# K and Q stored as three rows per dimension, head packs loaded by one transfer, and the reciprocal broadcast cut in four, with another order table

## The chip, the cores and the metric

The kernel runs on one core of a Trainium2 chip. The metric is the time of one execution on the device in microseconds (us). The version before takes 1923.54 us, the median of three runs (1922.4 to 1924.5). Beside the runs stands one execution that was recorded with the hardware profiler; all durations of single instructions come from it. Engines are named as the profile names them: PE multiplies matrices (PEld is its loading of weights), DVE is the vector engine, ACT the scalar engine, POOL the third elementwise engine, and SP only issues transfers (DMAs). All DMAs of this kernel are issued by SP, one after the other; SP also does the waiting for them.

## The reference

The input x has 2048 rows (positions) of 640 numbers. The result is the sum of x, an attention block and a mixer block, both on the row-normalized x. Cut to what matters:

```python
xn = layernorm(x)
# attention, 32 heads of 20 dimensions
q, k, v = split(xn @ wqkv)
p = softmax(q @ k.T * 20 ** -0.5)
a = concat_heads(p @ v) @ wo
# mixer
h  = gelu(layernorm(xn) @ w1)            # four groups of columns shifted by +1, -1, +2, -2 positions
x1 = xn + shifted(h) @ w2
b  = x1 + gelu(layernorm(x1) @ w3) @ w4  # w3: 640 x 1536
return x + a + b
```

Everything is float32. The kernel multiplies with a shortened float32 type and so writes each operand as a high part plus a low part; a product is high*high + high*low + low*high.

## The kernel before

**Work.** Heads go in 16 pairs, and each pair in two blocks of 1024 queries, which makes 32 blocks. For a block, PE forms the scores twice: `pm` with queries on the partitions, over whose rows DVE takes maxima (`mx`), and, once the maximum is known, `s` with keys on the partitions, which ACT turns into `p` by the exponential. PE multiplies `p` with V (`pv`), whose output also holds the sums of `p`. All else (projections to K, Q and V, the mixer's four matrices, preparing weights, the final product with wo) is laid between the blocks' steps, so that PE has work when ACT or DVE lag.

**K and Q on their way.** A projection of 128 columns comes out of PE as `ps_k` or `ps_q`, is split into `hl` = (high, low), a tile of 128 x 2 x 512 with two buffers, and is stored to DRAM (`kd`, `qd`). A pack is what PE reads for a pair: `kpack` (two buffers, 2048 keys) and `zq` (three buffers, 1024 queries). Head e of the pair has partitions 64e to 64e+59: 20 dimensions, each three times. `SLOT_K` = (0, 0, 1) and `SLOT_Q` = (0, 1, 0) say which part stands in which of the three places: high, high, low for K, and high, low, high for Q, so that one product over 60 partitions makes the three terms at once. Two more partitions take the maxima (`zq<-md`). In the version before the three places are three blocks of 20 partitions, and `load_k` issues a DMA for each of them; `load_q` issues one for the first two and one for the third. A head that lies across two groups of 128 columns is loaded in two pieces, each by three DMAs.

**The sums.** At a block's end (`block_end`) the sums of `p` go to DRAM (`od<-ob`), come back spread over 128 partitions (`sm<-od`), DVE takes reciprocals (`rc`), which go to DRAM (`rcd<-rc`) and come back to every partition that needs them (`rb<-rcd`); POOL multiplies, and four DMAs store the result (`onm<-rb`).

**What sets the order.** A planner (`Plan.schedule`) runs over all operations with assumed costs and writes out a fixed order for each engine. The table `ORDER` decides what PE takes next: s (a score product), p (a product with V), m (a maximum product, counted apart only at places), d (anything that is due). A DMA has in the plan an issue cost on SP, a time `xfer` on one shared path, 1600 ns until it has landed, and an allowance `late` (3000 ns for prepared weights, `PREP`, and for the sums' chain, `LATE`; 1500 ns for packs). Eight DMAs may be under way; the ninth waits for the first. Engines take their instructions strictly in the planned order.

**Preparing weights.** `prep` loads a piece of a weight matrix (`ph_w<-in`), rounds it on ACT or DVE (`ph_w<-ph_w`), subtracts on POOL, and stores both parts (`wd_w<-ph_w`); later a DMA brings them to where PE reads them (`w_w<-wd_w`, `xT<-wd_w`). These casts stand in ACT's row between the exponentials.

Of the kernel before, what the change touches and what calls it, by code (L numbers as in the profile page):

```python
# [88 lines left out]
LATE = 3000.0  # L89
KB = 1  # L90
# [21 lines left out]
    "dsdsdddssppppssdsdddssdddssdddssddsddddsdsdddsddsdsddsdsdppppsddssddsdssddsdddsdsdsdddddsdsdsdppsssppdsddsdddd"
    "ddddsddsdddsssddddsddssddsddsdsdsddsdsppppssddsdsddsdsddsdddsdsdsddssddsdsddsdddssppppssdddssddsdsddddsdsddsdd"
    "ssdddsdsdsdsddpppssddddsddsdsddsdsddsdsdddddsspssdsdsdsdsddppppsddsddssddssdssdddddssddsdsdspssdppsspdssddsdsd"
    "psdddddsdsddddsddsdddssdddsddsddsdddsdsdddsdspppssddsddsddsddssddsdsdddsdsdppppsdsddsddsdsdsdddssdsdddddsddsds"
    "dsddsdsppppsdsddssdddsdssddddssddsdddssdsddsdsddspssspssddddsddsdddsdppdsdddssdsdsdsdsdsdsdddssppppssddsdsdsdd"
    "dsspdpssddddsdspdsdsdddsdpsddssdddssdsddsdsddsdddssddsdsdddssppppssdddssddsddsddsdsdsddddsssddddddsdssdddsdsdd"
    "sdsdppppssddsddsddsddsdssddsdddsdssddsppppsdsdsddsdsddsdsdddsddsdsdssdsdsdsddsdddssdpdpppsddssddssddsdsddsdsdd"
    "spssddpsdsppsdsdsddsdddsddddsdddddsdddsssdddddsdsddssdddssddsdsdppsssppsdsdsdsdddsdsddsdsdsdsddsdsppppsdsddsds"
    "dsdddsdsddsddsdsdddsdddsdsdsddsdspdpppssddddsdssddsdsddsdsddsdsdddsdsdsdsppppdsdssdddsdsddsdsdsdddddsssdddddsd"  # L120
    "ssdddsddsddsdsdpssspppddsdsddddddssddsdsdddssdddsdssddsddssppssdddsdsdddsspsspssspssspssspssspdssspssspssspsss"
    "pssddddsddsddddsdddddsssddddsdddddddsddsddddsddddsdddddsddsddppppsdsdddssdddsddsddddddddsddsddddsdddddddssdddd"
    "dsddddddddddsdsdddddsppppsdddsddddddsssdddddddsdsdddddddsddddddddsddppdddsddddsddddsddddsddsdddsdsdddsddddddds"
    "ppsddsdddddsddsddddsddssdddsdsdddsdsdddsddddddddddssddddpppsspssdddsdddsddsddddsdddssdddddsdddsdddsddddppsssps"
    "sspsddddsddsdddsddddsddssdddsdddsdddsdddsddddsdddddsddsppsssddppssdsdddddddsspddspssssspdpsdsdsddsdsdddddsddsd"
    "ddsssddddsdddddsdsdsddddddddsdsddsdddsdssddddpppppsdddsdsddddsdddddddsdddddsdsdddsddsddddssdddsddddsdsdddsddsd"
    "dspppsddddddsdsddddsddddssdddsdsddssdddsdsddsddssdppppssddsddsddssdddsdsdsdsdddssppppdsddsdssdddsdddssddsdddsd"
    "ddsdsddsddsdsdsddsdsdddsspppssdddsddsddsddsddsddsddsppppsddddsddddsdddsdsdddspsdsddssddsddsddssddsdsddsdsppsss"
    "ppdsdsddssdddssdddssdddsddssdsddsddsdsppppdsdsdsdsddsdsdddsdddsdsddsdsdsddsdsdsddsdsppppdssddsddsdsddsdsdsddds"
    "ddsddsddsddsdsdsdddsdddssdppppdsdddsddsdsdsdddsdsddddsdsdsddsdsddsdsppppsdsddssdddssdsddsddsddsddssdddsddssddp"  # L130
    "pppddsssddddsdsdsddsdddddsssddddsddssdddsdsdsddddssssppssppsssspssspssspssspsddsdsdddddsdsdddsdddssddsdddddsdd"
    "ssddddddssppppsdsddsdsdddddsddsddddssdsddddsddsddddsdddsdsppdsddddsddsdddsdddsdddsppsddsddsdsddddssddddddsddds"
    "ddddddsddddddssdddddddsdsdddddddddddddddsddppppdsdsddsdddddsdsdddddssddddsddsddsdddsddddssppppsdsdsdsdddsddddd"
    "sdsdddssddsddsdddddsdddsdddddddddssddpppddsdddddddsddsdddddsdpsdsdsdddsdddsdddsddsddsdddsddsddddsddddsdspssddp"
    "sddsdsddsdddsddsdddddsdddddddsdsppspssspssddpssspdsdddsddddsspsspddsssssspssspssddddsdsddssdddsdsdsddsdsppsdsd"
# [476 lines left out]
def tile_kernel(tc, x, wqkv, wo, w1, w2, w3, w4, out):  # L612
# [1002 lines left out]
```

## Time and profile before

| | |
|---|---|
| median of three runs | 1923.54 us |
| the profiled execution | 1928.14 us |
| its span, first to last instruction | 1926.4 us |
| PE busy | 97% of the span |
| DVE, ACT, POOL busy | 79%, 72%, 23% |
| mean granted clock of PE | 0.981 |
| DMA issues | 1355 |

PE's busy share is near the whole span, so what counts is where PE stands still and where its clock is lower than 1.00. A row of the view by stretches gives: the stretch (us from the span's start), its length, busy us of PE, PEld, DVE, ACT and POOL with their instructions, PE's granted clock, the DMA engines' mean busy share, and GB/s. A row of the chain of waits gives start, length and what the time went to; "DMA a<-b" there is the time from a DMA's issue to its landing as far as the next step waited for it. A row of the timeline gives start, length, engine, operation, tiles and count, and in brackets how long the engine stood idle before it and what ended that.

### The profile page before, as it was taken

The numbers are of one execution on the slowest core, as the hardware profiler recorded it, in microseconds if no ns is written. First come the engines' busy times: TensorE is split into PE (matmuls) and PEld (weight loads), VectorE is DVE, ScalarE is ACT, GpSimd is POOL, SyncE is SP. The second block draws the span as 40 slices with busy tenths as digits, with TensorE's granted clock in tenths as the row PEclk, the third lists the DMA queues.
The fourth block names the chain that finished last, engine by engine and source line by source line (L and its number), as shares of the span: only waits on it lengthen the run. The fifth ranks groups of instructions, "written<-read, shape, count | busy, mean of one in ns | idle before, by whom it ended". The sixth has DMA issues, their size and how long they took to land.

```text
span 1926.4 us, 44100 instructions
## 1 busy us (share of the span) xinstructions
PE 1861.3 (97%) x17153; PEld 1295.4 (67%) x17153; DVE 1512.6 (79%) x2691; ACT 1382.0 (72%) x2540; POOL 446.2 (23%) x663
## 2 busy tenths in 40 slices
PE   8999999998989999899999989999999999999998
PEld 7976676665665646566665757656677777776677
DVE  8998678886878888877778986768788877878734
ACT  5278667886877886668778666867777777777762
POOL 5012123423412333211111221101112222221211
PEclk9999999999999999999999999999999999999999
DMA  5664546536444586544424452233622323253502
GB/s 187 180 180 153 133 119 191 142 125 180 120 134 123 154 248 195 182 132 158 149 83 140 148 174 98 92 93 111 168 86 73 113 69 106 72 149 102 163 17 110
DMA packets 229425, 257.78 MB, mean 134 GB/s; under 512 B 57784, under 2 KB 172936, under 8 KB 229216
## 3 DMA queue, kind: packets, MB, share of 16 engines
q1 hardware_dynamic: 229216, 254.96, 44.3%
q8 instruction: 135, 2.21, 0.5%
q14 instruction: 74, 0.61, 0.1%
HBM read 151.64 MB, written 103.25 MB: 132 GB/s over the span
## 4 chain that ended last, share of the span: by engine, by line
PE 81%; DMA 10%; DVE 4%; ACT 2%; SPq 1%; issue 1%; POOL 1%; DVEq 0%; ACTq 0%; POOLq 0%
PE ps L356 23%; PE pv L356 20%; PE s L356 12%; PE pm L356 12%; PE psv L356 3%; PE pso L356 3%; DVE mx L324 3%; PE ps_q L356 3%; PE ps_k L356 3%; DMA kpack<-kd 2%; DMA ph_w<-in_B_w_dram 2%; SPq L324 1%; PE psl L356 1%; DMA zq<-qd 1%; DMA od<-ob 1%
## 5 line engine op out<-in xcount | busy, mean ns | idle before, releaser
L324 DVE TENSOR_REDUCE mx<-pm 128x1 f32<-128x512 f32 x2048 | 1271.3, 682 | 220.6 <-PE pm L356 127.2
L324 ACT ACTIVATE p<-s 128x512 f32<-128x512 f32 x2048 | 1109.1, 604 | 214.5 <-PE s L356 104.1
L356 PE MATMUL s<-zq,kpack 62*128 62x512 f32 x2048 | 759.0, 413 | 25.4 <-ACT p L324 10.9
L356 PE MATMUL pm<-kpack,zq 60*128 60x512 f32 x2048 | 761.8, 412 | 19.8 <-ACT p L324 13.4
L356 PE MATMUL pv<-p,v 128*32 128x512 f32 x4096 | 487.7, 601 | 2.8 <-ACT p L324 2.5
L356 PEld LDWEIGHTS s<-zq,kpack 62*128 62x128 f32 x2048 | 365.0, 188 | 131.8 <-DVE mx L324 33.1
L356 PEld LDWEIGHTS pm<-kpack,zq 60*128 60x128 f32 x2048 | 368.0, 188 | 117.5 <-ACT p L324 28.8
L356 PE MATMUL ps<-xT,w_w 64*128 64x512 f32 x2040 | 344.0, 401 | 5.4 <-DMA w_w<-wd_w 5.4
L356 PEld LDWEIGHTS pv<-p,v 128*32 128x32 f32 x4096 | 120.4, 109 | 237.2 <-issue 202.4
L356 PEld LDWEIGHTS ps<-xT,w_w 64*128 64x128 f32 x2040 | 222.8, 191 | 41.8 <-issue 10.4
L324 POOL TENSOR_TENSOR ob<-ob,obq 128x512 f32<-128x512 f32 x96 | 124.0, 1292 | 324.4 <-ACT obq L324 291.3
L356 PE MATMUL ps<-xT 64*128 64x320 f32 x1632 | 172.8, 308 | 0.0
L356 PEld LDWEIGHTS ps<-xT 64*128 64x128 f32 x1632 | 147.6, 186 | 12.1 <-issue 2.1
L324 ACT COPY obq<-pv 128x512 f32<-128x512 f32 x85 | 50.0, 588 | 129.4 <-PE pv L356 128.8
L356 PE MATMUL ps<-xT,gT 64*128 64x320 f32 x1152 | 123.1, 307 | 0.0
L344 POOL MEMSET scratch<- 1x1 f32 x134 | 12.3, 92 | 454.8 <-PE ps L356 273.7
L356 PEld LDWEIGHTS ps<-xT,gT 64*128 64x128 f32 x1152 | 104.8, 186 | 9.0 <-issue 3.4
L356 PE MATMUL psv<-wv,xT 64*128 64x320 f32 x960 | 93.9, 314 | 0.0
L356 PEld LDWEIGHTS psv<-wv,xT 64*128 64x128 f32 x960 | 83.3, 190 | 7.2 <-POOL scratch L344 1.4
L356 PE MATMUL ps_q<-xT,w_q 64*128 64x512 f32 x480 | 81.1, 398 | 0.0
L356 PE MATMUL ps_k<-xT,w_k 64*128 64x512 f32 x480 | 80.6, 399 | 0.0
L356 PE MATMUL pso<-wos,oT 64*128 64x320 f32 x768 | 67.0, 308 | 0.0
(180 smaller groups left out, 1382.4 us busy)
## 6 DMA issues: line engine op xcount, KB each, us to landing
kpack<-kd SPq DMA_DIRECT2D x78, 160.0 KB
w_w<-wd_w SPq DMA_DIRECT2D x48, 256.0 KB
gd<-pre SPq DMA_DIRECT2D x8, 1536.0 KB
g<-gd SPq DMA_DIRECT2D x64, 192.0 KB
wd_w<-ph_w SPq DMA_DIRECT2D x34, 320.0 KB
xT<-wd_w SPq DMA_DIRECT2D x34, 320.0 KB
zq<-qd SPq DMA_DIRECT2D x52, 160.0 KB
vd<-vst SPq DMA_DIRECT2D x32, 256.0 KB
```

Of the source, the lines that this page charges most:

```text
L324: o.insts = [getattr(e, m)(val(out), *[val(x) for x in ins], **{k: val(v) for k, v in kw.items()})]
L344: o.insts = [nc.gpsimd.memset(scratch.get(), 0.0)]
L356: o.insts = [nc.tensor.matmul(out.get(), lhsT.get(), rhs.get(), **kw) for out, lhsT, rhs, kw in products]
```

## The change

1. **Layout in DRAM.** `qd` and `kd` get the shape (128, 3, 2048): the three rows of a dimension stand next to each other in the order that the pack wants. `keep` stores a piece with two DMAs: one for both parts, and one that stores the high part a second time.
2. **Packs.** Partition 3*o + slot instead of 20*slot + o. A head is loaded by one DMA of 60 rows, a head across two groups by two. `place`, which builds the first pair's pack on the chip, is filled with step 3.
3. **Reciprocals.** `rb<-rcd` is four DMAs of 32 partitions each, every one from one row of 512.
4. **The planner's assumptions.** `dma` is told over how many DMA engines it spreads (`on`: for a pack the largest number up to 16 that divides its rows, 4 for `od`, 10 for `onm`); some issue costs and element sizes are other ones. The allowance for packs has a name and the same value.
5. **ORDER** is another table with the same counts of letters (4479 d, 2005 s, 512 p, 43 m). Of its rows two stand below.

```diff
+RLATE = 1500.0
 ORDER = (
...
-    "psddsddddddsssddddsddddddsddsdddddsddddsdddsdssdddddssdddddssddddsddddsdsdppppdsdsdsdddsddddsdddddsssdddddddsd"
+    "pdsddsdddddsssdddddddddssdddsdddddsdddsddddsddsdsdddssddddsddddsddsddsdsddppppsddsddddssddddsdddddsssddddsddds"
...
-    def dma(o, i, nbytes, es=2560, iss=None, **kw):
+    def dma(o, i, nbytes, es=2560, iss=None, on=16, **kw):
...
-                 xfer=1.1 * (8.0 + 0.0375 * es) * math.ceil(n / 16), **kw)
+                 xfer=1.1 * (8.0 + 0.0375 * es) * math.ceil(n / on), **kw)
...
-                b = 64 * h + slot * DH
-                pl("pool", 110.0, "tensor_copy", place[:, e, part, b:b + DH], ident[:, h * DH:(h + 1) * DH])
+                b = 64 * h + slot
+                pl("pool", 110.0, "tensor_copy", place[:, e, part, b:b + 3 * DH:3], ident[:, h * DH:(h + 1) * DH])
...
-    qd = [dt([P, 2, 2, HALF], F32R, f"qd{c}") for c in range(ND)]
-    kd = [dt([P, 2, 2, HALF], F32R, f"kd{c}") for c in range(ND)]
+    qd = [dt([P, 3, S], F32R, f"qd{c}") for c in range(ND)]
+    kd = [dt([P, 3, S], F32R, f"kd{c}") for c in range(ND)]
+    def keep(dst, k, tb, hl):
+        c = slice(tb * 512, (tb + 1) * 512)
+        dma(_f(dst[:, 1:3, c] if k else dst[:, 0:2, c]), _f(hl), 524288, 2048, 430.0)
+        return dma(_f(dst[:, 0 if k else 2, c]), _f(hl[:, 0, :]), 262144, 2048, 390.0)
...
-            dma(_f((qd, kd)[e][0][:, tb // 2, :, tb % 2 * 512:tb % 2 * 512 + 512]), _f(hl), 524288, 2048, 560.0)
+            keep((qd, kd)[e][0], e, tb, hl)
...
-                    for slot, part in enumerate(SLOT_K):
-                        b = 64 * e + slot * DH + o
-                        rdma(_f(t[b:b + n, s]).rearrange("p (c t) -> p c t", c=2), _f(src[r0:r0 + n, :, part, :]), n * S * 4, 4096)
+                    b = 64 * e + 3 * o
+                    rdma(_f(t[b:b + 3 * n, s]), _f(src[r0:r0 + n, :, s]).rearrange("p s t -> (p s) t"), n * S * 12, 8192, on=span(3 * n))
...
-                slots = list(enumerate(SLOT_Q))
-                if n == DH:
-                    b = 64 * e
-                    rdma(_f(t[b:b + 2 * DH, :]), _f(src[r0:r0 + n, qh]).rearrange("p q t -> q p t"), n * HALF * 8, 4096)
-                    slots = slots[2:]
-                for slot, part in slots:
-                    b = 64 * e + slot * DH + o
-                    rdma(_f(t[b:b + n, :]), _f(src[r0:r0 + n, qh, part, :]), n * HALF * 4, 4096)
+                b = 64 * e + 3 * o
+                rdma(_f(t[b:b + 3 * n, :]), _f(src[r0:r0 + n, :, qh * HALF:(qh + 1) * HALF]).rearrange("p s t -> (p s) t"),
+                     n * HALF * 12, 4096, on=span(3 * n))
...
-        adma(rb, rcd[blk].unsqueeze(1).to_broadcast([4, 32, 512]), 262144, LATE)
+        for r in range(4):
+            adma(rb[32 * r:32 * (r + 1), :], rcd[blk, r:r + 1].to_broadcast([32, 512]), 65536, LATE, iss=450.0)
```

What this does to the order of instructions shows best on SP. A row gives line, operation, the tile written and the tile read with their numbers, the shape written (partitions first), and xN for equal rows that follow each other.

SP before, where the packs of blocks 3 and of the second pair's K are loaded (`zq1`, `kpack0`), with the weight pieces `ph_q3` around them:

```order
L324 DMA ph_q3_0_3474<-in_A_wqkv_dram 128x2x128
L324 DMA zq1_79<-qd0_100 40x1x1024
L324 DMA zq1_79<-qd0_100 20x1024
L324 DMA zq1_79<-qd0_100 40x1x1024
L324 DMA zq1_79<-qd0_100 20x1024
L324 DMA ph_q3_1_3511<-in_A_wqkv_dram 128x2x128
L324 DMA kpack0_76<-kd0_105 20x2x1024 x6
L324 DMA vd1_111<-vst2_217 128x8x64
```

SP with the change, the same place:

```order
L325 DMA ph_q3_0_3489<-in_A_wqkv_dram 128x2x128
L325 DMA zq1_79<-qd0_100 60x1024 x2
L325 DMA kpack0_76<-kd0_105 60x2048 x2
L325 DMA ph_q3_1_3547<-in_A_wqkv_dram 128x2x128
L325 DMA vd1_111<-vst2_217 128x8x64
```

Ten pack DMAs became four of 60 rows, and `ph_q3_1` now stands behind all of them instead of ahead of the K packs.

ACT before, the cast of that piece of weights among the exponentials (`p67_0` is the one of step 67 for head 0):

```order
L324 ACTIVATE p66_0_3550<-s66_0_3587 128x512
L324 ACTIVATE p66_1_3560<-s66_1_3595 128x512
L324 CAST ph_q3_1_3511<-ph_q3_1_3511 128x256
L324 ACTIVATE p67_0_3561<-s67_0_3603 128x512
L324 ACTIVATE p67_1_3562<-s67_1_3617 128x512
L324 ACTIVATE p68_0_3563<-s68_0_3635 128x512
```

ACT with the change:

```order
L325 ACTIVATE p66_1_3566<-s66_1_3602 128x512
L325 ACTIVATE p67_0_3567<-s67_0_3616 128x512
L325 ACTIVATE p67_1_3568<-s67_1_3621 128x512
L325 ACTIVATE p68_0_3569<-s68_0_3638 128x512
L325 CAST ph_q3_1_3547<-ph_q3_1_3547 128x256
L325 ACTIVATE p68_1_3575<-s68_1_3655 128x512
```

The cast moved behind three more exponentials. In the whole row of ACT most such casts stand at the same step as before or within ten steps of it.

SP before, the reciprocals of block 0 (`rb0`) and the stores of Q (`qd1<-hl_q1`):

```order
L324 DMA rcd_125<-rc0_255 128x16
L324 DMA ph_q2_2_3036<-in_A_wqkv_dram 128x128
L324 DMA ph_k3_0_3049<-in_A_wqkv_dram 128x2x128
L324 DMA rb0_256<-rcd_125 128x1x512
L324 DMA wd_q2_2_175<-ph_q2_2_3036 256x1x128
L324 DMA qd1_101<-hl_q1_2_2956 128x2x512
```

SP with the change:

```order
L325 DMA rcd_125<-rc0_255 128x16
L325 DMA ph_q2_2_3047<-in_A_wqkv_dram 128x128
L325 DMA ph_k3_0_3062<-in_A_wqkv_dram 128x2x128
L325 DMA rb0_256<-rcd_125 32x512 x4
L325 DMA wd_q2_2_175<-ph_q2_2_3047 256x1x128
L325 DMA qd1_101<-hl_q1_2_2968 128x512
L325 DMA qd1_101<-hl_q1_2_2968 128x2x512
```

One broadcast became four, and each store of Q or K became two. Over the program SP issues 1333 DMAs where it issued 1355: 68 `zq<-qd` instead of 152, 34 `kpack<-kd` instead of 102, 120 `rb<-rcd` instead of 30, and 80 stores to `kd` and `qd` instead of 40.

More of the change, by code (lines that the diff above doesn't have):

```diff
@@ new lines @@
+    "ddmdddmdddddmdddmddddddmddddmddddddddddddddddmdddddmdddddddmmdddddddddmddddddddddmdddddmddddddmmddddddmddddddd"
+    "dddddddddmddddddddmmdddddmddddddddddmddddddddddddmdddmmdddddddddddddddmddddddddmddddddddmdmdddddddmdddddddddmd"
+    "ddddddddddddmsdddddddddsdddsddsdddddsddsddddsdsddddssddsddddssddddsddmddddddsddsdsdmddsppppsdsdsdsdddssdsdddsd"
+    "dsddssddsdsddsddsmppppssdddssddsddsddsdsdsdsdddssdddssddsddmdsppsspdsdsddsddsddspssddddsdsddssddsddsdsdddssppp"
+    "psddssdsddsdddsdsddssdddssdpssspppsddssdddssdddssdddsddddsssdddsdddssddsdsddsdsppssdddspsssppssspdsddsdddsddsp"
@@ new lines @@
+    "dsdssddsdsppppsddsdsddsdsdsdsddsdsddsddsdsddddsdsddddsdsppppsdsdddssdsdsddsdsdsddsddddsddsdddssppssppdsdddsddd"
+    "dsdddddsdsddssddddsddssdddssddsdsdddssppppsdsdsdddsdsddsdsddssdddsdssddsddsdsdddssppppssdddssdsddsdddsdddssdsd"
+    "dsdddsdsdsdsdsdpppsdsdddsdsdddsddsddsdsdddddsspssdsddsdsdsddppppdsdsddssdssdddsdsdsdddssddsspsdspssppdssdsddsd"
+    "psdddddsdddsdsdddsdddssdddsdsdddsddsdsdddddsspppdssdsdddsddsdsdsddsdsdddssdppppssdddsdsddsdsddssdddsdsddsdddsd"
+    "sddsdsppppsdsddssddsdddssddsdsdsdddsdsdsddsdsddsdspssspssdddsdddsdddsppdsddddsdssdsdsdsdsddsdsppppsdsdsdsdddss"
@@ new lines @@
+    "ddsdppssdddddsspdsdsddddsspdssddsddssddsdddsdsdsddsddssdddssdppppssdddsdsddssdddssddsdsdddssdddsddsdsdsdsddsds"
+    "ppppsdsdddsddsddddssddsdddsdssdddssddsppppssddsddsddssddsdddsdddsddsssdsddssdsddsdsdppppdsddsdsssdsddssdddsdsd"
+    "dssdddspsspppssddsddsddddddsdddddsddddsssdddsdsddsdsdddsddsddsdsppsssppssdddsdsdsddsddsdsdsdsdddssppppssdddssd"
+    "ddsdsddsdsddsdsddddddsdsdsdsddsdspdpppssdddsddssdsddsdsdddsddssddsdsddsdsppppsddsddddsdsddsdsdsddddsssdddddsds"
+    "ddsdsddsdsddsdspssspppsdsddddddsddsddsdsdsddssddddsdsdsdsddsppsdsddsdsddsspsspssspssspssspdssspssspssspssspsps"
@@ new lines @@
+    "ddsddssdddddsdsdddddssdsddddddssddddsdddddsddsddddsdddsddsdddppppdsdddssddddsddsddsddddddddddsdsdsddddddssdddd"
+    "ddddssddddddddddsddsddppppdsdddsddddsssddddddsdddsdddddddddsdddddsddppddsddddsdddddsdddddsdsddddsddddsddddddss"
+    "ppsddsdsddddddsddsdsdddssdddsdddddssdddsddddsddddddsddddppppssdddsddddsddddddddsdsddsddddssddsddsddddspsssppss"
+    "spsdsdddsddddssdddsddsddsdddsdssdddddsddddddsddddsddddspppsssddsppsdddsdddddsssddpssssspdpdsdsddsddddsddsdsddd"
+    "dsssddddsddssddsdddsdsddddsddddssdsddsdddddddspppppsdsdddsdsdddsdddsddsdddddsdddsddsdddddddssdddsddsddsddsdddd"
@@ new lines @@
+    "ddddpppsddssddddsdddddddssddsdsdddssdsdddsddssddsdppppssdddsdsddssddsddsdsdsdddssppppdsdsddssddsdsddsddsdsddsd"
+    "dsdddsdsddsdsddsdsddsdddsspppssddddsddsddsdsddsddsddsppppddssdddddddsddsdddsdspsdsddsdsddsddsdssdddsdsddspsssp"
+    "ppsddsdsdsddsdsddsddsdsdddssddsdsddsdsppppdsdsddsdsdsddsddddsddsddsdsdsddsdsdsddsdsppppsdsddssddsddsdsddsdsdsd"
+    "ddsdddsddsdsdsdsddsdsdddsdppppddsddsdsdsdsddsdddsdsdddsddsdsddsdsppppsdsddsddsdsddssddsddsddsdsddssdddsdsdsddp"
+    "pppsddsdssddsddddssdsdddddsssdddsddsddsdddssdddddsssspppsspsssspssspssspssspssdddsdsdddsddsddddddssddsddddsdds"
@@ new lines @@
+    "dsdddsdddsppppsdsddsdsddddsddddsdddssddsdddddsddssdddsdddsppddsdddsddddsddsddddsdsppssddddssddddddsddsdddsdddd"
+    "dsddsddddddddssdddddddsdsdddddddddddddddsddppppsddsdddddsdsdddddsddssdddsdddddsdsddsddsddsppppssdsddddsdddsdsd"
+    "sdddddssddddddsdssdddsddddsdddddddsddpppddsddddddsdsddddddssddpdssddsdddsdddsdsddddddddsddsdddsddsddddsdspssdd"
+    "pssdddddssdddsdsdddddsdddddddsdsppspssspssddpsspssddsdsdddddspsspddsssssspssspsdddsdsdsddddsssdddsdddssppsdsdd"
+    "dsdsdddddsdsdddddsdddsdsdddsdsdddsddsdppppdddssddddsddddsddddddsdddsddsddsddsddsdddssdddddsddddssddddddddddddd"
@@ new lines @@
+    "dsdddddssddppppssdddddssddppsddsdsddddsdsdddsddddsdsdsdddsdddsssdddsddsdddsddsddssdddsppsssppsdsdsddsddssdddss"
+    "ddsdsdddsspppsddsdsddsdsddsdsddsddsddspdpppsddsdddddsdddsdsddddsspssdddssddsdsdddssddsdsddsdsppppsdsdsddsdsdds"
+    "ddssdddsdddsssddddsddsdsdsdsddsdsddsdppppsdsdsdsdddssdddsdsdsdsdddssppssddddsdsdddsdsddsdsddddsddsddsdddsppppd"
+    "ddsdsdddsdsppsdsdsddsddsddsdsddsddssddddsdddsdsddssddsdsddddssppppsdsdsdsddsddsdsddsdsdddddsdsddsdsdsddsdspppp"
+    "ssddsdsdddssddsddsddssdddssdddsddsdspssspssspsssppdsspssspsddsdddddsdspsddsddsdddsdddsdsddsdddddsdsdddspsddsdd"
@@ new lines @@
+    "ddpppssddddsdddsdddddddsddddsdsddddsdsdsddddddsdddddsdddddddddssddsddddddddddsdddddsddddsddddsdsdppppsdsddddds"
+    "dddssddsddddsdddsdddssdddddssdddddsdddsdsdppppsdddsddsddddsdddsdddsddsddsddsddsdddddddsdssdddsddppppdsddsdsdds"
+    "ddsdddddsddsddsdsddsdddsddddsdddssdddsddddssppppssddddddsddsdsdddsddddsdddsdsddddsddddsddsdsdddsdsdppppsdsddsd"
+    "dddsdddssddsddddsddddssdddddsddssdddddsddssddppppsddsdddssdddddssdddddddsdsddsdddddsdsddddsdsddddssdppppdsdsds"
+    "ddsdddddsddddsddsdsddddsdsdddddsddsdsdsdddddssdppppdssdddsdddsdsddsdddddsddsddsddsdddsdddsddsdddsdddsdsppppssd"
@@ new lines @@
+    "dddsdddsddsdddsdsdddsddsddddssdddddsdsddddsddsdsdppppsddsdsdsddddsddddsdsddsddsdddddsdddsdddsddssdddddsdsdpppp"
+    "sddsdsddddssdddsdddsdddsddsddddsddsdsdddsddsddsddddssppppsddsdsdddsdsdddsdddsddsddsdddsddsddddsdddssdddsdddsds"
+    "ppppsddsddsdsdddsdsddddsdsddddsdddsdddsddsddsddsddsdddsdsppppssdddsdsdddddsddddsdsdddsddddsdsdsddddddssdppppsd"
+    "ddsddddsssddddddsdsddddsdsdddddsdsddsdddsdsddddsddsddsdddsdsppppsdsddddsdsddddsdsdddddsdsdsddsddddddsdsddsdsdd"
+    "ddsdsdppppssdddsddddsdddssdddsdsddddddsddssddddddsdssdddsdddsdppppsddsdsddddssdddddsdddsdsddddsdsddddsdddssdpp"
@@ new lines @@
+    "ppdsdsddddsddssddddssddddsdsdddsdddddsdsddsddddsddsdsdddsddddsdsdppppsddsdddsdsdsddddsddddssdddddsddsdsdddddsd"
+    "sdddsdsdddsppppsddsdsdddsddddsddsddsdddsddddssddsdddddsdsddsddddssdppppssdddsdddsddsddsdddsddddsddsddddssdddds"
+    "sdddppppsddsdddddsssddddddsddsdsddddsddddssddddddssdsddddddsdsdddsdsdppppsddsdsdddsddddsdsdddsdddsdsdsdddddsdd"
+    "sddsddsddddssddppppsddsdsdsddddsddddssdddddsddsdddssdddsddddsdsddsddddssppppssddsddddsddsdddsddsdddsdsddsddsdd"
+    "ddsdsppppdsddsddssddddddssddsddddssddddsddsdddsddddsddssdddsddddssppppsddsddsdddsdddddddsddddssdddddsddsddsdsd"
@@ L779, in prep @@
         w = dt([P, 2, n], F32R, "wd_" + name)
-        dma(_f(w), _f(hl[:, :, :n]), n * 1024, 8 * n if n == 320 else 4 * n, 480.0).late = PREP
+        dma(_f(w), _f(hl[:, :, :n]), n * 1024, 8 * n if n == 320 else 4 * n, 430.0 if n == 320 else 600.0).late = PREP
         wdone[name] = w
@@ L1008, in qk_tile @@
                 split_ps(hl[:, 0], hl[:, 1], ps, 512, (st1, 1))
-                kept[nm, tb] = dma(_f(dst[:, tb // 2, :, tb % 2 * 512:tb % 2 * 512 + 512]), _f(hl), 524288, 2048, 560.0)
+                kept[nm, tb] = keep(dst, nm[0] == "k", tb, hl)
     def v_half(h, vp, w):
@@ L1372, in tile_kernel, with span, adma @@
     fill["on"] = False
-    def adma(o, i, nbytes, late=0.0, es=2048, iss=None):
+    def span(n):
+        return max(k for k in range(1, 17) if n % k == 0)
+    def adma(o, i, nbytes, late=0.0, es=2048, iss=None, on=16):
         k = pl.key
         pl.key = k + K_DMA
-        r = dma(o, i, nbytes, es, iss)
+        r = dma(o, i, nbytes, es, iss, on)
         r.late = late
@@ L1381, in adma, with rdma @@
         return r
-    def rdma(o, i, nbytes, es=2048):
-        adma(o, i, nbytes, 1500.0, es)
+    def rdma(o, i, nbytes, es=2048, on=16):
+        adma(o, i, nbytes, RLATE, es, on=on)
     def rows(src, head):
@@ L1503, in block_end @@
         n = 2 * HALF // P
-        adma(od[blk], ob[DH:P:32, :], 8192, LATE, 2048, 600.0)
+        adma(od[blk], ob[DH:P:32, :], 8192, LATE, 2048, 600.0, 4)
         pl.key += REST
@@ L1516, in block_end @@
             c0 = qh * HALF + r // 2 * 512
-            adma(onm[h * DH:(h + 1) * DH, c0:c0 + 512], rb[32 * r:32 * r + DH, :], 40960)
+            adma(onm[h * DH:(h + 1) * DH, c0:c0 + 512], rb[32 * r:32 * r + DH, :], 40960, on=10)
     def normed(qh, pool):
```

80 lines of the change are left out of this document (15 added, 65 removed).

## The prediction

> **What bounds the kernel now.** First the busy times by engine, then the stretches of the span, then the chain of waits and the timeline at the places that the stretches point to.
>
> ```profile
> PE 1861.3 (97%) x17153; PEld 1295.4 (67%) x17153; DVE 1512.6 (79%) x2691; ACT 1382.0 (72%) x2540; POOL 446.2 (23%) x663
> ```
>
> PE is the bound over the whole, but the mean hides where its time is lost.
>
> ```profile
> 0.00:200.00 200.00, 193.91 (x1775) 151.91 (x1777) 177.30 (x337) 118.81 (x232) 52.43 (x128) 0.99 0.57 173
> 200.00:1400.00 1200.00, 1146.51 (x9876) 763.60 (x9874) 950.37 (x1679) 893.96 (x1638) 272.78 (x386) 0.97 0.49 144
> 1400.00:1750.00 350.00, 350.00 (x3706) 257.04 (x3707) 283.65 (x486) 265.41 (x475) 83.87 (x81) 1.00 0.33 93
> 1750.00:1926.40 176.40, 170.84 (x1812) 122.89 (x1804) 101.23 (x192) 103.79 (x197) 37.13 (x68) 1.00 0.31 102
> ```
>
> From 1400 to 1750 PE works without a gap at the full clock, packs being loaded there too. Between 200 and 1400 it stands for 1200 - 1146.51 = 53.5 us, and its granted clock is 0.97. Cut finer, almost all of that lies in thirteen short stretches:
>
> ```profile
> 205.00:220.00 15.00, 10.93 (x92) 8.45 (x86) 6.86 (x12) 7.04 (x15) 2.04 (x3) 0.77 0.56 140
> 262.00:276.00 14.00, 11.82 (x116) 9.84 (x110) 8.46 (x14) 8.39 (x18) 2.70 (x4) 0.88 0.45 119
> 331.00:345.00 14.00, 12.18 (x84) 8.25 (x78) 7.70 (x15) 7.80 (x16) 3.34 (x3) 0.88 0.65 200
> 440.00:458.00 18.00, 12.91 (x86) 5.27 (x84) 8.82 (x16) 8.14 (x17) 2.22 (x3) 0.81 0.78 204
> 555.00:573.00 18.00, 12.25 (x92) 7.83 (x91) 9.58 (x19) 8.11 (x17) 0.00 (x0) 0.81 0.59 166
> 605.00:625.00 20.00, 16.56 (x132) 12.05 (x128) 13.49 (x23) 12.30 (x26) 2.66 (x3) 0.91 0.47 145
> 680.00:696.00 16.00, 13.93 (x100) 8.52 (x93) 10.46 (x18) 9.56 (x16) 2.81 (x3) 0.89 1.09 329
> 720.00:738.00 18.00, 15.46 (x154) 10.63 (x151) 11.02 (x22) 9.22 (x19) 3.97 (x6) 0.91 0.45 135
> 795.00:812.00 17.00, 11.77 (x112) 9.36 (x108) 9.73 (x17) 8.87 (x18) 1.75 (x3) 0.80 0.68 220
> 845.00:860.00 15.00, 12.25 (x105) 7.43 (x103) 5.46 (x9) 6.65 (x13) 2.77 (x4) 1.00 0.32 102
> 915.00:938.00 23.00, 20.39 (x142) 12.73 (x140) 13.97 (x22) 16.66 (x25) 2.42 (x3) 0.85 0.63 216
> 1140.00:1160.00 20.00, 14.50 (x88) 8.75 (x82) 12.37 (x23) 10.35 (x22) 0.00 (x0) 0.83 0.57 164
> 1270.00:1286.00 16.00, 11.91 (x83) 7.50 (x77) 6.75 (x12) 8.10 (x16) 0.00 (x0) 0.79 0.43 118
> ```
>
> Length less PE busy, summed, is 224.0 - 176.9 = 47.1 us of standing. The clock takes more: (1 - clock) times PE busy, row by row, adds to 25.0 us, since after most of the gaps PE runs slowly for a while. Together 72.1 us.
>
> Who is late there, the chain of waits tells:
>
> ```profile
> 95.15 2.54 DMA zq<-md
> 201.95 11.28 DMA ph_q<-in_A_wqkv_dram
> 262.37 7.63 DMA ph_w<-in_B_w_dram
> 675.90 6.61 DMA qd<-hl_q
> 782.33 13.37 DMA kpack<-kd
> 795.77 6.15 DMA wd_w<-ph_w
> 801.98 2.77 DMA ph_w<-in_B_w_dram
> 845.62 9.06 DMA ph_w<-in_B_w_dram
> 907.15 11.71 DMA zq<-qd
> 1258.01 12.33 DMA kpack<-kd
> ```
>
> A DMA with free engines lands in 2.5 to 2.8 us (the rows at 95.15 and 801.98), the same kind in 6 to 13 us behind packs. The timeline of SP and then of ACT shows how that becomes a stall:
>
> ```profile
> 779.70 2.59 SPq L324 DMA_DIRECT2D zq<-qd  x4
> 782.33 8.96 SPq L324 DMA_DIRECT2D kpack<-kd  x6
> 794.81 0.35 SPq L324 DMA_DIRECT2D v<-vd  x1
> 804.82 0.46 ACT L324 CAST ph_w<-ph_w 128x320 fp32r<-128x320 f32 x1 [5.79 <-DMA ph_w<-in_B_w_dram]
> ```
>
> SP issues four Q packs and four K packs, waits with eight under way, and comes past the packs at 794.81, 15 us after their start. What stands behind them on SP is late by that, here the weight piece whose cast stands in ACT's row ahead of exponentials: ACT idles 5.79 us, no `p` is made, the PSUM buffers stay full, PE stops.
>
> **The change part by part.** *Packs.* Moved bytes are the same for a pair: per head 160 + 80 KB of Q and 3 x 160 KB of K, 1440 KB for both. What changes is how many DMA engines share them.
>
> ```profile
> 207.00:213.00 6.00, 3.19 (x37) 2.67 (x35) 3.77 (x6) 1.10 (x3) 1.29 (x1) 0.99 0.38 94
> 676.00:692.00 16.00, 13.93 (x107) 8.24 (x107) 11.41 (x21) 12.14 (x20) 5.33 (x5) 0.96 1.05 331
> ```
>
> With packs under way the engines are busy 0.38 on average and move 94 GB/s; with weights of 128 rows 1.05 and 331 GB/s. So the old packs leave most engines empty and keep a few full. The program's shapes say why that should end: the Q pack reads 2 x 20 rows into 40, the new one 60 into 60. The Trainium skill, page "DMA: Bandwidth & Descriptors", section "Why a DMA increments its semaphore by 16 and not by 1", has a transfer run on the largest number of engines up to 16 that divides the slowest dimension of both sides: 2 for the first of a head's old Q transfers, 10 for the other old ones, 15 for the new; the 0.38 agrees.
>
> At 331 GB/s times 15/16 the 1440 KB take 4.6 us, the 480 KB of a block without K 1.5 us. What is issued right behind a full load then lands after at most 4.6 + 2.8 = 7.4 us instead of 11.3 to 13.4, and behind Q packs alone after 4.3 instead of 7.6 to 9.1. That is 4 to 6 us and 3 to 5 us earlier, about as much as PE stands in each row (1.8 to 5.8 us). I therefore take the losses as gone in the nine rows with a DMA share under 0.65. In the four others (331, 440, 680, 795: 0.65 to 1.09) transfers beside the packs fill the engines too; their losses of 3.3, 7.5, 3.6 and 7.6 us I count half gone, so 11.0 us stay. Gain 72.1 - 11.0 = **61.1 us**; the bounds are 72.1 and, if each loss shrinks by half, 36.
>
> On the clock the rows disagree with themselves: 2.18 us of standing at 262 came with 0.88, 2.75 us at 845 with 1.00. The Trainium skill ("TensorE: Matmul & The Clock Gate", Part 1) has the clock fall after an idle window of some 3.4 us and advises against gaps over 3 us. By that rule gaps cut to half would give back the whole 25 us of clock; the row at 262 says no, and the row decides.
>
> *SP.* Issuing costs SP time, not PE:
>
> ```profile
> L324 SPq DMA_DIRECT2D kpack<-kd x102: 583/739/1199, 71.0 to 1690.8; - x102
> L324 SPq DMA_DIRECT2D zq<-qd x152: 242/464/950, 44.8 to 1736.8; - x152
> L324 SPq DMA_DIRECT2D kd<-hl_k x16: 365/387/887, 126.6 to 629.4; - x16
> L324 SPq DMA_DIRECT2D rb<-rcd x30: 567/588/881, 173.6 to 1809.2; - x30
> ```
>
> By the medians, 68 K packs and 84 Q packs fewer free 50.3 + 39.0 = 89 us; 40 stores more cost 15.5 us, 90 broadcasts more at 387 to 588 ns 35 to 53 us. SP ends 21 to 39 us lighter, most of that at the packs. I add nothing to the gain for it, since the queue's share is in the rows above.
>
> *Stores.* 40 more of 256 KB take 0.8 us each at 331 GB/s and hold one of two `hl` buffers longer by that and an issue of 0.39 us: 0 to 40 x 1.2 = 47 us if every one were on the path. The cover is the other buffer and the work of blocks between; I take 2 us. If it is gone, the next `ps_k` or `ps_q` stays in PSUM and PE waits.
>
> *Broadcast.* The path from sums to `onm` is needed at a block's end plus some steps, and POOL is 23% busy; faster or slower by 3 us it stays covered: 0.
>
> *Order.* Counted in the tables, PE enters and leaves runs of p 407 times instead of 419.
>
> ```profile
> PEld pv L356 <- issue: 202.4, 669, 0.7
> ```
>
> A weight load of `pv` waits 202.4/669 = 0.30 us at a turn, so 12 fewer are worth 0 to 3.6 us; since matmuls before cover some of it, 1 us. `place` writes as many columns as before: 0.
>
> Sum: -61.1 + 2 - 1 = -60.1 us. The profiled execution took 1928.14 us (span 1926.4), so the same execution would take 1868.0; it lies 4.6 us over the median of 1923.54, and the median becomes 1863.4: **1863 us**.
>
> **The rivals.** *A: the stalls shrink but stay.* Then half of the 72 us returns, 1923.5 - 36 = 1888. For it: the new order takes three exponentials more ahead of a cast, but puts that weight piece behind the K packs too; and DVE is near its limit in the stage around 750, so that PE's gaps there would be filled by waiting for `mx`:
>
> ```profile
> 750.00:800.00 50.00, 49.81 (x526) 34.76 (x519) 49.15 (x102) 35.96 (x72) 16.82 (x22) 1.00 0.63 197
> ```
>
> Against it: in all thirteen rows DVE is busy 67% of the stretch or less. Chance 0.15.
>
> *B: full engines stop everything (slower).* Now some engines stay free beside packs; with 15 of 16 taken, every small transfer waits for the whole load, the maxima (`zq<-md`) and sums too, and they have less slack than weights. There are 15 pair loads. If each held PE for the full 4.6 us and the clock took 2 more, as after such gaps now, that is 99 us against the 72 lost today: 1923.5 + 27 - 1 = 1950. It decides from 72/15 = 4.8 us lost at a pair load. For it: at 680 full engines went with a gap of 2.07 us. Against it: those transfers stood behind the old packs as well, for longer. Chance 0.08.
>
> *C: the packs don't go faster*, the 60 rows being taken by as few engines. Then only SP's issues are saved: of the 15 us of a pair load, two zq and four kpack issues, 2 x 0.46 + 4 x 0.74 = 3.9 us. A quarter of the 72 us at most, 18: 1905. The 4.6 us need 331 GB/s, which the trace shows for 128 rows and not for 60. Chance 0.03.
>
> **How the numbers follow.** Forecast 0.74, A 0.15, B 0.08, C 0.03. The range goes from 1844 (all 72.1, the 3.6 of the turns and some 4 of the 6.3 us of other standing between 200 and 1400) to 1890, which takes in A; C and B lie outside. Changes below 0.2%, 3.8 us, can't be told from none. Faster has the forecast, nearly all of A and most of C, 0.89; the same 0.03; slower B, 0.08.
>
> **What would show it.** Right: rows of stretches between 200 and 1400 with PE near full and clock 1.00; DMA share near 1 for some 5 us at a pair load; no chain piece of `kpack<-kd` or `zq<-qd` over 8 us; ACT's waits for `ph_w` far below the present ones. Wrong: the same gaps with `kpack` landing in 3 us, which would mean that the planned slack, not the packs, made them; DVE's waits taking their place (A); or waits for `zq<-md` that weren't there (B).

## The result and the profile after

The changed kernel takes 1848.91 us (median), the one before in the same comparison 1924.02 us: a ratio of 0.9601, 95% interval 0.9576 to 0.9627. It is 75.1 us faster; the forecast was 1863 us with a range of 1844 to 1890. One of its four executions took 3898.34 us at a granted clock of 1.00, for a reason that nothing here shows; the ratio leaves it out, and without it the median is 1847.58 us.

Where PE loses time, by the busy line of the page and the same stretches of the span as shown of the version before:

```profile
PE 1832.6 (99%) x17153; PEld 1274.3 (69%) x17153; DVE 1506.6 (82%) x2687; ACT 1377.6 (75%) x2535; POOL 450.4 (24%) x672
0.00:200.00 200.00, 194.21 (x1775) 149.39 (x1777) 177.26 (x337) 117.36 (x229) 55.75 (x131) 0.99 0.63 194
200.00:1400.00 1200.00, 1195.98 (x10706) 801.06 (x10706) 1007.73 (x1782) 950.34 (x1740) 297.80 (x415) 1.00 0.51 154
1400.00:1750.00 350.00, 349.46 (x3598) 248.33 (x3592) 284.67 (x489) 267.89 (x489) 82.79 (x88) 1.00 0.36 109
1750.00:1848.50 98.50, 92.96 (x1085) 75.53 (x1082) 36.97 (x81) 42.02 (x81) 14.07 (x39) 1.00 0.19 68
```

Between 200 and 1400 PE now stands for 1200 - 1195.98 = 4.0 us instead of 53.5, and its granted clock is 1.00 instead of 0.97. At the start and from 1400 on it stands as long as before, to within 0.6 us. For the same 17153 instructions PE is busy 1832.6 us instead of 1861.3. The times of two of the thirteen stretches with stalls (other work falls there now), and two loads of a pair's packs, of the changed kernel in the same columns:

```profile
205.00:220.00 15.00, 15.00 (x160) 10.40 (x154) 10.36 (x18) 11.49 (x24) 2.12 (x3) 1.00 0.83 207
440.00:458.00 18.00, 18.00 (x156) 12.55 (x156) 15.64 (x29) 14.20 (x27) 6.92 (x11) 1.00 0.69 229
310.00:320.00 10.00, 10.00 (x87) 9.10 (x85) 9.32 (x16) 9.09 (x18) 3.18 (x6) 1.00 1.00 263
735.00:745.00 10.00, 9.85 (x110) 6.33 (x109) 9.94 (x24) 6.33 (x14) 3.66 (x4) 1.00 0.95 254
```

Beside these two loads (first K pack at 311.0 and 736.9) the DMA engines are busy 0.95 to 1.00 and PE works through. Over 10 us at each of twelve pair loads the engines are busy 0.70 to 1.01, and PE 9.64 us or more. The chain that ended last contains these DMAs between 200 and 1848 us:

```profile
420.14 8.64 DMA hsd<-hlh
629.37 8.28 DMA kpack<-kd
637.71 7.95 DMA qd<-hl_q
648.51 6.26 DMA sm<-od
738.80 11.09 DMA ph_w<-in_B_w_dram
```

They are five instead of 25 in the same view of before, but these landings are not short: 8.28 us for a K pack, 11.09 us for a weight piece behind packs. What became short is SP's way past them. The timeline of SP at one and the same pair load (the one ahead of `v<-vd` near a third of the program), first before, then after:

```profile
542.51 2.39 SPq L324 DMA_DIRECT2D zq<-qd  x4
544.94 6.59 SPq L324 DMA_DIRECT2D kpack<-kd  x6
555.21 0.36 SPq L324 DMA_DIRECT2D v<-vd  x1
...
561.24 1.28 SPq L324 DMA_DIRECT2D ph_w<-in_B_w_dram  x2
```

```profile
521.01 0.77 SPq L325 DMA_DIRECT2D zq<-qd  x2
521.83 0.84 SPq L325 DMA_DIRECT2D kpack<-kd  x2
...
525.91 0.41 SPq L325 DMA_DIRECT2D v<-vd  x1
...
531.68 0.94 SPq L325 DMA_DIRECT2D ph_w<-in_B_w_dram  x2
```

From the first Q pack to the issue of the next weight pieces SP took 561.24 - 542.51 = 18.7 us, and now 531.68 - 521.01 = 10.7 us. (The order between the two changed as well; e3 below has the same order and the old spread.) The view of SP's own waits tells what held it: it waited 81.9 us for Q packs to land before (29 times, 4.3 us at most), and 2.4 us now (4 times).

### The profile page after: what moved, and what is told of

The parts are those of the page before. It is cut to its first block, busy times and chain, and to the rows that moved or that the text cites. A ratio compares the mean times of both kernels' runs of the same rounds, so it can differ in the third digit from the quotient of the medians.

```text
span 1848.5 us, 44129 instructions
## 1 busy us (share of the span) xinstructions
PE 1832.6 (99%) x17153; PEld 1274.3 (69%) x17153; DVE 1506.6 (82%) x2687; ACT 1377.6 (75%) x2535; POOL 450.4 (24%) x672
## 4 chain that ended last, share of the span: by engine, by line
PE 92%; DMA 3%; DVE 2%; ACT 1%; POOL 1%; issue 0%; SPq 0%; DVEq 0%; ACTq 0%; POOLq 0%
PE ps L357 26%; PE pv L357 24%; PE s L357 14%; PE pm L357 14%; PE psv L357 4%; PE pso L357 3%; PE ps_k L357 3%; PE ps_q L357 3%; DVE mx L325 1%; PE psl L357 1%; DMA ph_w<-in_B_w_dram 1%; ACT p L325 0%; DMA hsd<-hlh 0%; DMA kpack<-kd 0%; DMA qd<-hl_q 0%
## 5 line engine op out<-in xcount | busy, mean ns | idle before, releaser
L357 PE MATMUL pm<-kpack,zq 60*128 60x512 f32 x2048 | 753.2, 407 | 2.6 <-ACT p L325 1.7
L357 PEld LDWEIGHTS s<-zq,kpack 62*128 62x128 f32 x2048 | 360.4, 185 | 104.4 <-issue 29.0
L357 PEld LDWEIGHTS pm<-kpack,zq 60*128 60x128 f32 x2048 | 361.7, 185 | 99.2 <-issue 28.9
L357 PE MATMUL ps<-xT,w_w 64*128 64x512 f32 x2040 | 330.5, 393 | 0.1
L357 PEld LDWEIGHTS pv<-p,v 128*32 128x32 f32 x4096 | 117.8, 109 | 237.5 <-issue 211.0
L357 PEld LDWEIGHTS ps<-xT,w_w 64*128 64x128 f32 x2040 | 209.5, 187 | 36.0 <-issue 2.9
L357 PE MATMUL ps_q<-xT,w_q 64*128 64x512 f32 x480 | 79.3, 395 | 0.0
```

The source lines that it names most:

```text
L357: o.insts = [nc.tensor.matmul(out.get(), lhsT.get(), rhs.get(), **kw) for out, lhsT, rhs, kw in products]
```

## The experiments

Theory T: the old packs ran on few DMA engines, which made them slow, and with them all that SP issues behind. Its rivals: the new order alone took the stalls away (O), or the smaller number of issues did (I). Each group of runs has its own runs of the kernel before: 1927.12 us with e1 to e4, 1927.72 with e5 to e8, 1927.25 with e9 and e10.

### e1: the new transfers under the old table

The changed kernel with the whole table of before; the diff is against the changed kernel and shows one of its rows.

```diff
 ORDER = (
...
-    "pdsddsdddddsssdddddddddssdddsdddddsdddsddddsddsdsdddssddddsddddsddsddsdsddppppsddsddddssddddsdddddsssddddsddds"
+    "psddsddddddsssddddsddddddsddsdddddsddddsdddsdssdddddssdddddssddddsddddsdsdppppdsdsdsdddsddddsdddddsssdddddddsd"
...
```

> The changed kernel with the ORDER table of before; transfers, layout and the planner's assumptions are the changed ones. Theory T (the packs on few engines made the stalls, and wider packs take them away): most of the 75 us stay won, 1848 to 1862 us, and few gaps between 200 and 1400. Rival O (the new table, with later places for what waits, took the stalls away): at least half of the gain is lost, over 1885 us, with PE standing where it stood before.

1862.84 us, ratio 0.9656 (0.9634 to 0.9679). So 64.3 us of the gain come without the new table. PE between 200 and 1400 in that run:

```profile
200.00:1400.00 1200.00, 1188.99 (x10556) 793.02 (x10554) 999.62 (x1765) 940.92 (x1724) 290.79 (x408) 1.00 0.51 154
```

11.0 us of standing are left there, against 53.5 before and 4.0 with the new table. Most of the gain stays, as T expected, though the time lies just over its upper end of 1862.

### e2: the new table over the old transfers

The kernel before with the whole table of the change; the diff is against the kernel before and shows the same row.

```diff
 ORDER = (
...
-    "psddsddddddsssddddsddddddsddsdddddsddddsdddsdssdddddssdddddssddddsddddsdsdppppdsdsdsdddsddddsdddddsssdddddddsd"
+    "pdsddsdddddsssdddddddddssdddsdddddsdddsddddsddsdsdddssddddsddddsddsddsdsddppppsddsddddssddddsdddddsssddddsddds"
...
```

> The kernel of before with the new ORDER table alone; transfers, layout and the planner's assumptions as before. T: no gain to speak of, 1910 to 1935 us, and the gaps behind pack loads stay. O: most of the gain is there, under 1880 us.

1954.45 us, ratio 1.014 (1.0116 to 1.0163): slower by 27.3 us. Neither theory had expected a loss. In the chain of waits the old pieces are back:

```profile
560.97 8.91 DMA kpack<-kd
795.24 13.40 DMA kpack<-kd
923.88 12.91 DMA zq<-qd
1151.93 13.12 DMA kpack<-kd
```

O falls: the table alone does not take the stalls away. With wide packs and the new assumptions it gains 14 us, with narrow ones and the old assumptions it loses 27; that it fits only transfers that come through is a reading of these two numbers, not shown.

### e3: the old spread under the new order

```diff
+CUT_Q = (38,)
+CUT_K = (50,)
...
+    def cut(r, o, i, at):
+        def fn():
+            for x, y in zip((0,) + at, at + (60,)):
+                r.insts = [nc.sync.dma_start(o.get()[x:y], i.get()[x:y])]
+        r.fn = fn
...
+                if n == DH:
+                    cut(r, o, i, CUT_Q)
```

The planner sees one transfer as before; only what is issued differs, so that PE, ACT, DVE and POOL keep the changed kernel's order.

> The changed kernel, every engine's order as it is there, but a whole head's Q pack goes in 38 + 22 rows and its K pack in 50 + 10 rows, so that a transfer spreads over as few DMA engines as it did before (a 40-row and 20-row piece then). T: the stalls come back, 1900 us or more, and the granted clock falls again. O (the order's slack is what counts): within 10 us of 1849.

1931.39 us, ratio 1.0011 (0.9992 to 1.003): the whole gain is gone. The stretch of the span, the chain and SP at the same pair load:

```profile
200.00:1400.00 1200.00, 1151.74 (x9983) 765.41 (x9982) 953.88 (x1688) 900.53 (x1649) 285.38 (x398) 0.98 0.50 150
```

```profile
206.88 9.30 DMA ph_q<-in_A_wqkv_dram
431.81 12.14 DMA kpack<-kd
549.20 14.28 DMA kpack<-kd
```

```profile
547.16 1.22 SPq L1400 DMA_DIRECT2D zq<-qd  x4
548.43 1.61 SPq L1400 DMA_DIRECT2D kpack<-kd  x4
552.83 7.05 SPq L327 DMA_DIRECT2D w_k<-wd_k  x3
...
561.78 0.35 SPq L327 DMA_DIRECT2D v<-vd  x1
...
565.34 1.67 SPq L327 DMA_DIRECT2D ph_w<-in_B_w_dram  x2
```

48.3 us of standing and a clock of 0.98. SP issues the eight pack pieces in under 3 us, with eight under way stops until 552.83, and needs 7.05 us for the next three issues, where the changed kernel takes 2.39 us. The weight pieces go out 18.2 us after the first pack, with the same order 10.7 us in the changed kernel. SP's waits for Q packs to land are back at 100.5 us. Stalls, clock and time return with every engine's order unchanged, so the cause lies in the transfers; whether in their spread or in their number, e4 tells.

### e4: as many issues as before, all wide

```diff
+CUT_Q = (30,)
+CUT_K = (15, 30)
```

> The changed kernel, same order, but a whole head's Q pack goes in 30 + 30 rows and its K pack in 15 + 15 + 30 rows: as many issues on SP as before the change (2 and 3 for a head), each still over 15 DMA engines. If the number of engines counts and not the number of issues, 1847 to 1855 us. If the issues on SP and the limit of eight under way count (rival I), a good part of the stalls is back: 1875 us or more.

1855.16 us, ratio 0.9622 (0.9599 to 0.9644). By the ratios that is 0.9622 - 0.9601 = 0.21% of the time before, about 4 us, behind the changed kernel, at the edge of what the intervals tell, and the time is at the upper end of 1855. I falls as the cause of the stalls: with 2 and 3 pieces for a head, but 15 engines for each, the gain stays but for these few us.

### e5 and e6: Q alone narrow, K alone narrow

Both against e3, first e5, then e6:

```diff
 CUT_Q = (38,)
-CUT_K = (50,)
+CUT_K = ()
```

```diff
-CUT_Q = (38,)
+CUT_Q = ()
 CUT_K = (50,)
```

> The changed kernel, same order on every engine, with only the Q pack of a whole head in 38 + 22 rows. The 38-row piece can share its work over 2 engines, as the 40-row transfer did before. Theory Q (the Q packs' two engines hold up all that follows): 1895 us or more, that is over half of the 82 us by which the kernel with both packs narrow was slower. Rival K (the K packs, three times the bytes per head, on ten engines): under 1870 us.

> The changed kernel, same order, with only the K pack of a whole head in 50 + 10 rows, ten engines each. Theory Q: under 1870 us. Rival K: 1895 us or more. If both matter by their sum, the two losses add to about 82 us.

e5 takes 1909.34 us (0.9909, 0.9879 to 0.994), e6 1867.76 us (0.9695, 0.9658 to 0.9731). Against 1848.91 the Q packs cost 60.4 us and the K packs 18.9 us, together 79.3, and both at once (e3) 82.5. Theory Q holds, and the losses add up within the spread of the runs. PE between 200 and 1400, e5 and then e6:

```profile
200.00:1400.00 1200.00, 1160.18 (x10114) 768.40 (x10112) 962.86 (x1704) 908.69 (x1665) 287.83 (x404) 0.98 0.51 150
```

```profile
200.00:1400.00 1200.00, 1186.29 (x10506) 790.01 (x10504) 991.75 (x1755) 936.52 (x1715) 295.42 (x409) 0.99 0.51 153
```

And what a narrow Q pack does to SP, in e5 at the pair load near 200 us:

```profile
197.58 1.46 SPq L1400 DMA_DIRECT2D zq<-qd  x4
199.09 0.79 SPq L1400 DMA_DIRECT2D kpack<-kd  x2
199.93 0.56 SPq L327 DMA_DIRECT2D ph_q<-in_A_wqkv_dram  x1
201.21 8.98 SPq L327 DMA_DIRECT2D vd<-vst  x2
210.28 3.22 SPq L327 DMA_DIRECT2D v<-vd  x1
```

After four Q pieces, two of them narrow, SP needs 8.98 us for the next two stores; in e9 below, where only the spread of the Q pieces differs, the same two take 1.99 us (at 201.51). The second of them waits until 205.8 for the first Q piece to land. A weight piece, `ph_q`, had gone out ahead of this stop, at 199.93, and is late all the same: ACT waits for it until 213.79, 13.9 us after its issue. In e9 it goes out at 200.78 and is used at 208.50, 7.7 us later. So narrow packs cost in two ways, a late issue and a late landing.

### e9: Q on ten engines

Against e5:

```diff
-CUT_Q = (38,)
+CUT_Q = (50,)
 CUT_K = ()
```

> The changed kernel, same order, with the Q pack of a whole head in 50 + 10 rows: as many issues as with 38 + 22, but ten engines each. If the number of engines is what costs, the 60 us of the 38-row piece shrink to a small part: 1849 to 1862 us. If cutting a Q pack in uneven pieces costs by itself (rival), 1880 us or more.

1846.69 us, ratio 0.9583 (0.9569 to 0.9598), just under the expected range: nothing is lost against the changed kernel. The same two issues for a head cost 60 us as 38 + 22 rows and nothing as 50 + 10. By the rule of the Trainium skill ("DMA: Bandwidth & Descriptors", section "Why a DMA increments its semaphore by 16 and not by 1"), the largest number up to 16 that divides the rows, 38 rows run on 2 engines and 50 on 10; this pair of runs agrees with that rule. The traces count the engines nearly directly: in their semaphore updates, which the views do not print, every transfer of 60 rows raises its semaphore in 16 steps, every one of 50 in 11, of 22 in 12, and of 38 in 3, as the old Q transfer of 40 rows does: by that rule one step more than engines, each time. e9 shows that the last five engines are not what counts for Q.

One wait that comes of it is that of ACT for weight pieces, shown for the kernel before, e5 and e9 (us in total, times, longest):

```profile
ACT ph_w L324 <- DMA ph_w<-in_B_w_dram: 22.8, 7, 5.8
```

```profile
ACT ph_w L327 <- DMA ph_w<-in_B_w_dram: 17.4, 6, 6.9
```

```profile
ACT ph_w L327 <- DMA ph_w<-in_B_w_dram: 4.7, 3, 1.9
```

In the changed kernel it is 3.4 us, and SP's waits for Q packs to land are 80.1 us in e5 and 3.8 us in e9.

### e7: one broadcast

The four are planned as before; one is issued for all, in the place of the last.

```diff
-        for r in range(4):
-            adma(rb[32 * r:32 * (r + 1), :], rcd[blk, r:r + 1].to_broadcast([32, 512]), 65536, LATE, iss=450.0)
+        four = [adma(rb[32 * r:32 * (r + 1), :], rcd[blk, r:r + 1].to_broadcast([32, 512]), 65536, LATE, iss=450.0) for r in range(4)]
...
+        def whole():
+            four[-1].insts = [nc.sync.dma_start(rb.get(), rcd[blk].unsqueeze(1).to_broadcast([4, 32, 512]).get())]
+        for f in four:
+            f.fn = None
+        max(four, key=lambda f: f.i).fn = whole
```

> The changed kernel, same order, with the four broadcasts of a block's reciprocals issued as the one of before (128 partitions from 4 rows). By the prediction the broadcast's path is covered: 1847 to 1852 us. If the narrow broadcast holds up what follows on the queue, as the packs did: 1860 us or more.

1846.77 us, ratio 0.9586 (0.9546 to 0.9627), just under the expected range. The four broadcasts bring and cost nothing that this interval, some 8 us to either side, can tell.

### e8: the added stores once more

```diff
+        def twice():
+            r.insts = [nc.sync.dma_start(_f(dst[:, 0 if k else 2, c]).get(), _f(hl[:, 0, :]).get())]
+            nc.sync.dma_start(_f(sink).get(), _f(hl[:, 0, :]).get())
+        r.fn = twice
```

> The changed kernel, same order, with the 40 stores of the second high row issued once more, to a place in DRAM that nothing reads. It prices the stores that the change adds. By the prediction 2 us (0 to 47): 1849 to 1853 us. If the stores are on the path, up to 1.2 us each: 1865 to 1896 us.

1852.26 us, ratio 0.9627 (0.9591 to 0.9663), 5.5 us over e7, which ran beside it and differs from the changed kernel by nothing that can be measured. That is about 0.1 us for each of forty more stores of 256 KB. The times of the two do not overlap (e7 up to 1849.93, e8 from 1851.78), the intervals of their ratios do: a few us are likely, and the 16 to 47 us of stores on the path are excluded.

### e10: the old assumptions in the planner

```diff
-                 xfer=1.1 * (8.0 + 0.0375 * es) * math.ceil(n / on), **kw)
+                 xfer=1.1 * (8.0 + 0.0375 * es) * math.ceil(n / 16), **kw)
...
-        dma(_f(dst[:, 1:3, c] if k else dst[:, 0:2, c]), _f(hl), 524288, 2048, 430.0)
+        dma(_f(dst[:, 1:3, c] if k else dst[:, 0:2, c]), _f(hl), 524288, 2048, 560.0)
```

The issue costs of the second store and of the prepared weights' stores, and the element sizes of two loads of weights, go back in the same way; the numbers given with the packs and with `rb` stay.

> The changed kernel with the planner's issue costs, element sizes and number of engines of before (16 everywhere); transfers and ORDER table are the changed ones. It tells whether the 14 us that the old table lost hang on the table alone. If the order tolerates such shifts: within 8 us of 1849. If table and assumptions only fit together: 1857 us or more.

1855.09 us, ratio 0.9632 (0.9614 to 0.965): 6.2 us behind, within what was expected of an order that tolerates shifts. So the old assumptions cost a few us of their own under the new table. e1 had the new assumptions, so its 14 us are the table's; e2 had the old ones, so part of its 27 us may be theirs.

## Why the prediction was right, and where its sizes were off

**The bound and the losses** were read rightly. 47.1 us of standing and 25.0 us of clock in the thirteen stretches went almost whole: standing between 200 and 1400 fell by 49.5 us, the clock of the long stretch is 1.00, and PE's busy time fell by 1861.3 - 1832.6 = 28.7 us for the same instructions. That the clock comes back with the standing counted: a third of what was lost there, 25.0 of 72.1 us, was not waiting but slow running beside it.

**The packs' term** was sized at 61.1 us. e1, which has everything but the table, gives 64.3, and e3 and e4 show that it is the spread. That the forecast left 11.0 us in four rows and that e1 still stands 11.0 us is chance: the first is standing and clock in four rows, the second is standing alone over 1200 us, 2.5 us of it between 775 and 790 and 1.7 between 1315 and 1325.

**The way to it was mis-sized in one step.** I let the 1440 KB of a pair's packs move at 331 GB/s times 15/16, in 4.6 us, and a transfer behind them land after at most 7.4 us. By the semaphore updates in the traces, the median over the 15 pair loads from the first pack's issue to the last one's landing was 18.6 us before and is 10.0 us now, more than twice the 4.6 (other transfers share these times); it is 15.0 in e5, 16.7 in e3 and 10.5 in e9. At the load near 200 us the weight piece behind the packs landed after 11.28 us before, and is used 8.2 us after its issue now (issue 201.64, cast at 209.88 without a wait), near the 7.4; at 738.80 one took 11.09 us, as long as before. So earlier landing is only a part of it. The other part is that SP, no longer held by slow Q packs with eight transfers under way (81.9 us of waits, now 2.4), issues what follows some 8 us earlier (18.7 and 10.7 us above). The prediction had that lag in its timeline (SP past the packs after 15 us) but put it into the rows and worked out landing times alone. How the gain divides between the two, no run takes apart. That the sum came out near 64 although this step was off is in part luck: the losses were taken as gone row by row, so the size of the step hardly entered it.

**The order's term** was taken at 1 us, from 12 fewer turns of PE. This term was mis-sized most: with the new transfers the table is worth 14 us (e1 against the changed kernel; by the ratios 0.9656 - 0.9601 = 0.55% of the time before, 10.6 us). It is not the turns that it wins by: PE's weight loads of `pv` waited 202.4 us in 669 turns before and wait 211.0 us in 705 now. It is the standing, 11.0 against 4.0 us, and the clock after it, 0.996 against 0.998 over the whole execution. Why this table does better than the old one, and so much worse with the old transfers, no run takes apart.

**SP's issues and the broadcast** were taken at nothing, and that held: about 4 us by e4, and none that e7 could measure. **The stores**, 2 us of a possible 47, lie in what e8 allows.

**The rivals.** The wait that adds up to most for DVE, before and then after:

```profile
DVE mx L324 <- PE pm L356: 127.2, 123, 5.2
```

```profile
DVE mx L325 <- PE pm L357: 106.3, 96, 3.4
```

A fell: no stall of that size took the old one's place, and the wait for `pm` is shorter, not longer. B fell: a pair load with engines at 1.00 leaves PE at 10.00 of 10.00 us, and PE waits for `zq<-md` once, for 0.6 us, as it did before for 0.7. C fell: the share of 0.38 with packs under way is 0.70 to 1.01 over twelve pair loads. One of the signs named for a right forecast did not come: a chain piece of `kpack<-kd` took 8.28 us, over the 8 us named, without a stall.

## What to carry to other kernels

Look at the shape of a transfer, not only at its bytes: 240 KB cut as 38 + 22 rows cost this kernel 60 us in 52 loads, and cut as 50 + 10 nothing, because what stood behind the slow pieces was issued late or landed late. Read SP's timeline from the first slow transfer to the first issue that someone waits for, and add the landing: that lag as a whole is what becomes a stall of an in-order engine three steps on. And an order that gains with one set of transfers can lose with another, here 14 us against 27: try table and transfers both apart and together.

## What was not expected of the hardware

At the pair loads, engines at 0.95 to 1.01 moved 254, 263 and 306 GB/s over 10 us, and 221 at 0.96 between 522 and 529, where weights of 128 rows had moved 331 GB/s at 1.05. Other transfers run in these stretches too, so what 60 rows move alone is not shown. And the cost of a slow transfer fell on its queue: in e5 SP needed 8.98 us for two stores of `vd` that read nothing of the packs, while in the changed kernel the K pack that took 8.28 us (issued at 629.37) left PE working without a gap:

```profile
625.00:640.00 15.00, 15.00 (x130) 10.17 (x130) 13.27 (x22) 11.70 (x22) 4.95 (x7) 1.00 0.93 246
```

On the clock the rows at 262 and 845 had disagreed. Cut at its edges, the row at 262 holds 3.41 us at a clock of 0.50 (270.86 to 274.27), behind 2.18 us of standing, and full clock otherwise. The changed kernel has one such spell left, 3.41 us at 0.50 from 752.26, behind 1.4 us of standing between 749.00 and that point. So in these traces a stop of 1.4 us was enough once, and one of 2.75 us at 845 was not; what decides between them is not shown.
